# Linear attention and MLP in one kernel: 64-token chunks from the fourth pair on, and a new order of loads, transposes and stores around it

## The chip, the cores and the metric

The kernel runs on one core of a Trainium2 chip. The metric is the device time of one execution in microseconds (us). PE is TensorE, DVE is VectorE, ACT is ScalarE, POOL is GpSimd; SP is the engine whose queue issues most of the transfers.

## The reference, cut to what matters

```python
# q, k, v: (4 batches, 8 heads, 768 tokens, 64); block = 64
for b in range(nb):
    intra = (q_b @ k_b.T * Dmask) @ v_b          # Dmask[i, j] = lam ** (i - j) for i >= j
    inter = (q_b * lam ** (pos + 1)) @ kv_state
    out_b = intra + inter
    kv_state = lam ** block * kv_state + (k_b * lam ** (block - 1 - pos)).T @ v_b
x = out, heads side by side                      # (4, 768, 512)
xn = (x - mean) / sqrt(var + 1e-6) * g_ln
y = x + relu(xn @ w_ch1) @ w_ch2                 # 512 -> 2048 -> 512
```

The block size is a choice of how to compute: any chunk length gives the same result, with more work inside the chunk and fewer states for a longer one.

## The kernel before, in words

The 3,072 rows are cut into 12 *pairs*, u = 0 to 11. A pair is a window of 256 tokens of one batch, two tiles of 128 rows (the index ab); pairs 0 to 3 are the first windows of the four batches, 4 to 7 the second, 8 to 11 the third. "u=3" is therefore the fourth pair. Each pair goes through attention, a norm and the MLP.

**Attention of a pair.** A load brings k, q and v of the pair, 512 KB each in float32. `in_k`, `in_q` and `in_v` cast them to bfloat16 (kq, vb) and scale q and v by powers of lam. kq is transposed to kqT, by PE for u=0 to 2 (`transpose_pe`) and by the DMA for later pairs (`transpose_dma`). Then come the scores (PE), a mask (DVE, mA), AV into the PSUM tiles po, and `inter`, which adds q times the state. The new states come from pk (k times v on PE, `kv` or `kv64`), which DVE sums with the old state and POOL decays to Sn.

**Two forms.** Pairs u < LB use 128-token chunks. Two neighbouring tokens (j) share a partition, so that one packet of a load is 512 B (line 71), and `scores`, `mask`, `av` and `new_state` do the work. Pairs u >= LB use 64-token chunks: loads of 256 KB in 256 B packets (line 75), `scores64` with half the columns, half as many AV matmuls (`av64`), and `states64`, with a state in mid-pair (Smid, cast to Sm by POOL). LB is 6. `rows_of` gives the matching order of the output rows.

**Norm and MLP.** `norm` copies po to x (ACT), takes mean and variance (DVE) and makes xc; `to_xT` transposes xc, from u=2 on by the DMA. An MLP group is one pair: eight `m1` blocks of eight matmuls (line 484) into a PSUM tile pm1, each followed by a relu on ACT (line 487), and eight `m2` blocks of four matmuls (line 522), and then DVE makes the output tile (`finish`, line 543) and SP stores it. [...]

**What sets the order.** Everything is written out by hand in a list `plan` of m1 and m2 blocks. Items 0 to 21 end the MLP of u=0 and u=1; group u=2 starts at item 22, u=3 at 38, u=4 at 54, and so on every 16. `add(n, steps...)` puts steps after item n, and each engine executes its instructions in that order. So do the DMA queues: an instruction on SP that waits holds all that stands behind it on SP. From u=7 on a fixed pattern repeats: `X(u)` holds AV and inter of u-1 and pk, scores and states of u, all at item 57 + 16 (u - 6).

Steps that the change touches: `fill` and `load_one` (loads), `p0` (casts of a pair), `transpose_dma`, `s1` to `s4` (the 128 form, cut into four places between MLP blocks), `X1` and `X2` (the handover from 128 to 64 at u=6), `wind_up` (AV and inter of a pair on its own, with a separate PSUM tile `rest`, till now only for the last pair), `p4` (the two xT transposes), `finish` (stores).

Of the kernel before, what the change touches and what calls it, by code (L numbers as in the profile page):

```python
# [8 lines left out]
BF16 = mybir.dt.bfloat16  # L9
I32 = mybir.dt.int32  # L10
ALU = mybir.AluOpType
# [5 lines left out]
def kernel(  # L17
# [11 lines left out]
    nc = tc.nc  # L29
    B, H, S, D = q.shape  # L30
    C = 128
    W = 2 * C

    NU = B * S // W
    DM = H * D
    DF = moe_w_ch1.shape[1]
    NP = H // 2
# [11 lines left out]
    wk = ctx.enter_context(tc.tile_pool(name="wk", bufs=2))  # L49
# [3 lines left out]

    half = [slice(0, 64), slice(64, 128)]
    XB = 3
    LB = 6

    def mm_tile(shape, dtype, name):
        return ps.tile(shape, dtype, tag="mm", bufs=4, name=name)
# [2 lines left out]
    qkv_in = {}  # L62

    def source(src, u, hs):
        cc, b = divmod(u, B)
        return src[b, hs, cc * W:(cc + 1) * W, :].rearrange("h (p j) d -> p h (j d)", j=2)

    def fill(got, name, u, hs):
        src = dict(k=k, q=q, v=v)[name]
        if u < LB:  # L70
            nc.sync.dma_start(got[:, hs], source(src, u, hs))  # L71
            return
        cc, b = divmod(u, B)
        for j in range(2):
            nc.sync.dma_start(got[:, hs, j * D:(j + 1) * D],
                              src[b, hs, cc * W + j * C:cc * W + (j + 1) * C, :].rearrange("h p d -> p h d"))

    def load_one(u, name):
        got = inp.tile([128, H, 2 * D], F32, tag=name + "in", name=name + "in")
        fill(got, name, u, slice(0, H))  # L80
        qkv_in.setdefault(u, {})[name] = got.rearrange("p h (j d) -> p h j d", j=2)

    def load_window(u, after_pool=False, parts=1):
        got = {name: inp.tile([128, H, 2 * D], F32, tag=name + "in", name=name + "in") for name in "kqv"}
        if after_pool:

            nc.gpsimd.memset(got["k"][:, 0, 0:1], 0.0)
        n = H // parts
        order = [(name, i) for i in range(parts) for name in "kq"] + [("v", i) for i in range(parts)]
        for name, i in order:  # L90
            hs = slice(i * n, (i + 1) * n)
            fill(got[name], name, u, hs)
        qkv_in[u] = {name: f.rearrange("p h (j d) -> p h j d", j=2) for name, f in got.items()}
# [77 lines left out]
    lam_p = const.tile([128, 2, H], F32)  # L171
# [4 lines left out]
    st = {}  # L176
# [12 lines left out]
    def part(a, dst, hs):  # L189

        return dst[:, a, hs.start // 2:hs.stop // 2].rearrange("p a j e d -> p a e j d")

    ALL = slice(0, H)
# [7 lines left out]
    def in_q(u, eng, hs=ALL):  # L201
# [7 lines left out]
        for j in range(2):  # L209
            eng.tensor_tensor(dst[:, :, :, j], src[:, :, :, j],  # L210
                              lq[:, :, :, j:j + 1].to_broadcast([128, n, 2, D]), op=ALU.mult)

    def in_v(u, eng, hs=ALL):
        n = hs.stop - hs.start
        lv = lam_v[:, hs, :, None] if u < LB else lam_p[:, 1, hs, None, None]
        eng.tensor_tensor(st[u]["vb"][:, hs], qkv_in[u]["v"][:, hs], lv.to_broadcast([128, n, 2, D]), op=ALU.mult)  # L216
# [7 lines left out]
                nc.tensor.transpose(tp[:, i, j, :], s["kq"][:, a, p, j], ident)  # L224
        (eng.tensor_copy if eng else nc.scalar.copy)(s["kqT"][:, a, pairs[0]:pairs[0] + n], tp)

    def transpose_dma(u):
        s = st[u]
        s["kqT"] = wk.tile([128, 2, NP, 2, 128], BF16, tag="kqT", bufs=3, name="kqT")
        for a in range(2):  # L230
            nc.sync.dma_start_transpose(s["kqT"][:, a].rearrange("p b j t -> p (b j) t"),
                                        s["kq"][:, a].rearrange("p b j e d -> p (b j e d)"))

    def scores(u, hf, early=False):

# [95 lines left out]
    def mask64(u, e):  # L331
        s = st[u]
        nc.vector.tensor_tensor(s["mA"][:, e], s["sc"][e],  # L333
                                keep64[:, None, None, :].to_broadcast([128, NP, 2, D]), op=ALU.mult)
# [132 lines left out]
    o_of = {}  # L467
# [61 lines left out]
    def rows_of(u):  # L529

        cc, b = divmod(u, B)
        order = "(c p j) d -> j p c d" if u < LB else "(j c p) d -> j p c d"
        return out[b, cc * W:(cc + 1) * W, :].rearrange(order, c=2, j=2)

    def finish(t, a):
        u, ab = divmod(t, 2)
        x, rstd = x_keep[u]
        cc, b = divmod(u, B)
        if ab == 0:
            o_of[u] = wk.tile([128, 2, DM], F32, tag="o", bufs=3, name="o")  # L540
        o = o_of[u]
        rows = rows_of(u)
        nc.vector.scalar_tensor_tensor(o[:, ab], in0=a, scalar=rstd[:, ab:ab + 1], in1=x[:, ab],  # L543
                                       op0=ALU.mult, op1=ALU.add)
        if u == NU - 1:
            for j in range(2):
                nc.sync.dma_start(rows[j][:, ab], o[half[j], ab])
        elif ab == 1:
            for j in range(2):
                nc.sync.dma_start(rows[j], o[half[j]])  # L550

    def finish_half(t, a, z, w):
        u, ab = divmod(t, 2)
# [138 lines left out]
    load_w2(3)  # L692
    in_v(2, nc.gpsimd)
    load_window(3, after_pool=True)
    load_window(4)

    def p0(u, k_eng=None):
        open_window(u)
        in_k(u, k_eng or nc.gpsimd)
        in_q(u, nc.gpsimd)  # L700
        in_v(u, nc.gpsimd)

    def s0(u):
        kv(u, "po")
# [15 lines left out]
    def wind_up(u):  # L720


        s = st[u]
        if u < LB:
            av(u, range(NP))
        else:
            av64(u)
        inter(u, 0, fence=False)
        qT = s["kqT"][:, 1]
        has = [s["S"][ab][1] is not None for ab in range(2)]  # L730
        rest = [ps.tile([128, H, D], F32, tag="sc", bufs=2, name=f"rest{ab}") if has[ab] else None for ab in range(2)]
        for p in range(NP):
            for jq in range(2):
                for e in range(2):
                    ab = 1 - e
                    if s["S"][ab][jq] is not None:
                        nc.tensor.matmul(rest[ab][half[jq], 2 * p + e, :], lhsT=qT[half[e], p, jq, half[ab]],
                                         rhs=s["S"][ab][jq][half[e], p, :],
                                         start=(p == 0), stop=(p == NP - 1), skip_group_check=True)
        s["x"] = xp.tile([128, 2, DM], F32, tag="x", name="x")  # L740
        s["mv"] = xp.tile([128, 2, 2], F32, tag="mv", name="mv")
        s["xc"] = wk.tile([128, 2, DM], BF16, tag="xc", name="xc")
        for ab in range(2):
            x, xh = s["x"][:, ab], s["x"][:, ab].rearrange("p (a e d) -> p a e d", e=2, d=D)
            nc.scalar.copy(x, s["po"][ab].rearrange("p h d -> p (h d)"))
            if has[ab]:

                odd = xh[:, :, 1 - ab]
                nc.vector.tensor_tensor(odd, odd, rest[ab].rearrange("p (a e) d -> p a e d", e=2)[:, :, 1 - ab], op=ALU.add)
            stats = wk.tile([128, 6], F32, tag="stats", name="stats")  # L750
            nc.vector.bn_stats(stats, x)
            nc.vector.bn_aggr(s["mv"][:, ab], stats)
            nc.vector.scalar_tensor_tensor(s["xc"][:, ab], in0=x, scalar=s["mv"][:, ab, 0:1], in1=g_row,
                                           op0=ALU.subtract, op1=ALU.mult)
# [59 lines left out]
    def X(u):  # L814

        if u - 1 < LB:
            av(u - 1, range(NP))
# [25 lines left out]
    def add(at, *steps):  # L843
        after.setdefault(at, []).extend(steps)
# [5 lines left out]
    add(6, (s2, 2))  # L850
    add(8, (s0, 2))
    add(10, (s3, 2))
    add(12, (s4, 2), (p4, 2), (p0, 3, nc.vector), (transpose_dma, 3))
    for n, name in zip((14, 15, 16), "kqv"):
        add(n, (load_one, 5, name))
    add(15, (rstd_of, 2))
    add(17, (p0, 4))
    add(25, (s1, 3))
    add(25, (transpose_dma, 4))
    add(27, (s2, 3))  # L860
    add(28, (p0, 5))
    add(29, (s3, 3))
    add(30, (s4, 3), (p4, 3))
    for n, name in zip((30, 31, 32), "kqv"):
        add(n, (load_one, 6, name))
    add(34, (rstd_of, 3), (make_keep64,))
    add(37, (transpose_dma, 5))
    add(38, (s1, 4))
    add(39, (p0, 6))
    add(40, (s2, 4))  # L870
    add(42, (s3, 4))
    add(44, (s4, 4), (p4, 4))
    add(46, (transpose_dma, 6))
    add(50, (s1, 5), (rstd_of, 4))
    add(53, (s2, 5))
    for j in range(6, NU):
        at = 55 + 16 * (j - 6)
        if j > 6:
            for n, name in zip((23, 21, 19), "kqv"):
                add(at - n, (load_one, j, name))  # L880
            add(at - 13, (p0, j))
            add(at - 8, (transpose_dma, j))
        if j < LB:
            add(at, (s1_s3, j))
            add(at + 4, (s2_s4, j), (p4, j - 1))
        else:
            if j == 6:
                add(at + 1, (X1, j))
                add(at + 5, (X2, j), (p4, j - 1))
            else:  # L890
                add(at + 2, (X, j), (p4, j - 1))
        add(at + 9, (rstd_of, j - 1))
    add(151, (wind_up, NU - 1), (p4, NU - 1))
    add(159, (rstd_of, NU - 1))
# [32 lines left out]
```

## Time and profile before

| | |
|---|---|
| time before, median of 3 | 215.92 us (214.59 to 216.27) |
| span of the profiled execution | 214.9 us |
| PE busy | 201.9 us, 94% |
| DMA, mean | 173 GB/s, 37.13 MB |
| loads of 512 KB, issue to landing | k 6.5, q 8.7, v 7.7 us (5 each) |
| loads of 256 KB, issue to landing | k 3.9, q 5.2, v 5.6 us (14 each) |
| transposes, issue to landing | xT 3.5 us (20), kqT 3.3 us (18) |

The granted PE clock is 0.996 over the span. On the page, a group of instructions has a line number, an engine, an operation, "out<-in" by the program's names and a count, then busy time and mean duration, then the idle time ahead of it and what ended it. A stretch view gives the busy time of each engine between two times. Matmuls are pipelined, so PE's busy time counts a matmul from issue to its modelled end, and neighbouring ones overlap.

### The profile page before, as it was taken

Reading aid. Unit: us, or ns where it says so; the run is one execution under the profiler, and the core shown is the slowest. Engines: PE = TensorE matmul, PEld = TensorE weight load, DVE = VectorE, ACT = ScalarE, POOL = GpSimd, SP = SyncE. Lnnn points to the kernel's source line nnn. Section 1 sums busy time; section 2 is a strip of 40 time slices with the busy share of each in tenths; the row PEclk is TensorE's granted clock in tenths of the full one; section 3 lists DMA queues with packets and bytes.
Section 4 is the critical chain, followed back from the end, with each engine's and each line's share of the span. In section 5 each row is a group of like instructions: output and inputs, shape, how many; then the busy total and the mean of one; then the engine's idle time right before and its main releaser. Section 6 shows DMA issues by size and latency. Waiting matters only on the chain.

```text
span 214.9 us, 6642 instructions
## 1 busy us (share of the span) xinstructions
PE 201.9 (94%) x2884; PEld 138.2 (64%) x2899; DVE 102.9 (48%) x225; ACT 87.1 (41%) x165; POOL 79.4 (37%) x111
## 2 busy tenths in 40 slices
PE   2989999999799999999999999999999999999992
PEld 0568788454674675585585685784784874866861
DVE  3678461565168436747347256174183292522011
ACT  4765679120442244055063162261370460731600
POOL 4747139039464173229019138056065020000000
PEclk9999999999999999999999999999999999999998
DMA  4999999999999898799799999998998511320303
GB/s 130 289 272 207 219 263 160 236 284 234 215 303 208 169 229 153 110 215 209 126 220 199 137 230 200 177 203 198 206 246 131 128 27 27 99 52 0 98 3 95
DMA packets 94142, 37.13 MB, mean 173 GB/s; under 512 B 68385, under 2 KB 91169, under 8 KB 94114
## 3 DMA queue, kind: packets, MB, share of 16 engines
q1 hardware_dynamic: 89584, 32.38, 71.4%
q0 software_dynamic: 4224, 4.19, 12.4%
q8 instruction: 22, 0.36, 0.7%
q10 hardware_dynamic: 306, 0.14, 0.3%
q14 instruction: 6, 0.05, 0.1%
HBM read 27.27 MB, written 6.29 MB: 156 GB/s over the span
## 4 chain that ended last, share of the span: by engine, by line
PE 75%; DMA 13%; POOL 4%; SPq 3%; DVE 2%; issue 1%; POOLq 0%
PE pm L484 35%; PE pm L522 30%; DMA vin<-in_v_dram 6%; DMA qin<-in_q_dram 4%; SPq L71 3%; DMA kqT<-kq 2%; POOL kq L210 2%; POOL vb L216 2%; PE pm2h L513 2%; PE po L406 1%; PE po L393 1%; PE sc L247 1%; PE po L380 1%; PE sc L327 1%; PE pm1t L496 1%
## 5 line engine op out<-in xcount | busy, mean ns | idle before, releaser
L487 ACT ACTIVATE hT<-pm 128x512 bf16<-128x512 f32 x92 | 54.9, 601 | 91.2 <-PE pm L484 91.0
L484 PE MATMUL pm<-xT,w 128*128 128x256 bf16 x736 | 86.3, 273 | 1.9 <-DMA xT<-xc 1.2
L522 PE MATMUL pm<-w,hT 128*128 128x512 bf16 x353 | 81.1, 379 | 1.0 <-issue 0.3
L484 PEld LDWEIGHTS <-w 128*128 128x128 bf16 x736 | 69.8, 98 | 13.8 <-DMA xT<-xc 1.7
L522 PEld LDWEIGHTS <-hT 128*128 128x128 bf16 x368 | 35.5, 98 | 40.0
L543 DVE SCALAR_TENSOR_TENSOR o<-pm,rstd,x 128x512 f32<-128x512 f32 x23 | 17.1, 748 | 43.5 <-PE pm L522 43.4
L287 POOL TENSOR_TENSOR Sn<-Stmp,lam_s 128x256 bf16<-128x256 f32 x16 | 9.7, 611 | 69.7 <-DVE Stmp L365 49.0
L435 DVE SCALAR_TENSOR_TENSOR xc<-po,mv,g_row 128x512 bf16<-128x512 f32 (+1 forms) x24 | 16.8, 706 | 1.8
L257 DVE TENSOR_TENSOR mA<-sc,keep 128x512 bf16<-128x512 f32 x20 | 13.1, 685 | 6.8 <-PE sc L247 6.7
L428 ACT COPY x<-po 128x512 f32<-128x512 f32 x18 | 9.9, 588 | 11.3 <-PE po L393 5.3
L430 DVE BATCH_NORM_STATS2 stats<-x 128x6 f32<-128x512 f32 x18 | 12.4, 688 | 3.9 <-ACT x L428 3.9
L417 DVE COPY seen<-po 128x8 f32<-128x8 f32 x18 | 2.3, 162 | 23.2 <-PE po L406 23.2
L216 POOL TENSOR_TENSOR vb<-vin,lam_v 128x1024 bf16<-128x1024 f32 (+1 forms) x7 | 11.8, 1696 | 3.7 <-DMA vin<-in_v_dram 3.7
L210 POOL TENSOR_TENSOR kq<-qin,lam_q 128x512 bf16<-128x512 f32 x10 | 10.3, 1045 | 7.0 <-DMA qin<-in_q_dram 7.0
L210 POOL TENSOR_TENSOR kq<-qin,lam_p 128x512 bf16<-128x512 f32 x12 | 12.3, 1042 | 0.9 <-DMA qin<-in_q_dram 0.7
L216 POOL TENSOR_TENSOR vb<-vin,lam_p 128x1024 bf16<-128x1024 f32 x6 | 11.4, 1896 | 1.7 <-DMA vin<-in_v_dram 1.7
L199 POOL CAST kq<-kin 128x512 bf16<-128x512 f32 (+1 forms) x18 | 10.3, 599 | 0.6 <-DMA kin<-in_k_dram 0.6
L333 DVE TENSOR_TENSOR mA<-sc,keep 128x512 bf16<-128x512 f32 x12 | 8.2, 681 | 1.4 <-PE sc L327 1.4
L406 PE MATMUL po<-Sn,kqT 64*64 64x64 bf16 x216 | 7.4, 199 | 0.0
L224 PE MATMUL tp<-ident,kq 128*128 128x128 bf16 x48 | 6.2, 277 | 0.3 <-ACT kq L199 0.2
L406 PEld LDWEIGHTS <-kqT 64*64 64x64 bf16 x304 | 5.3, 108 | 1.5 <-issue 1.5
L224 PEld LDWEIGHTS <-kq 128*128 128x128 bf16 x48 | 4.1, 120 | 3.2 <-DVE kq L199 1.5
(98 smaller groups left out, 146.0 us busy)
## 6 DMA issues: line engine op xcount, KB each, us to landing
out_dram<-o SPq DMA_DIRECT2D x22, 256.0 KB, 4.5
w<-in_moe_w_ch_dram POOLq DMA_DIRECT2D x8, 512.0 KB, 9.6
kin<-in_k_dram SPq DMA_DIRECT2D x14, 256.0 KB, 3.9
qin<-in_q_dram SPq DMA_DIRECT2D x14, 256.0 KB, 5.2
vin<-in_v_dram SPq DMA_DIRECT2D x14, 256.0 KB, 5.6
kin<-in_k_dram SPq DMA_DIRECT2D x5, 512.0 KB, 6.5
qin<-in_q_dram SPq DMA_DIRECT2D x5, 512.0 KB, 8.7
vin<-in_v_dram SPq DMA_DIRECT2D x5, 512.0 KB, 7.7
```

What stands on the lines that cost most here:

```text
L199: (eng.copy if eng is nc.scalar else eng.tensor_copy)(dst[:, :, :, j], src[:, :, :, j])
L210: eng.tensor_tensor(dst[:, :, :, j], src[:, :, :, j], lq[:, :, :, j:j + 1].to_broadcast([128, n, 2, D]), op=ALU.mult)
L216: eng.tensor_tensor(st[u]["vb"][:, hs], qkv_in[u]["v"][:, hs], lv.to_broadcast([128, n, 2, D]), op=ALU.mult)
L224: nc.tensor.transpose(tp[:, i, j, :], s["kq"][:, a, p, j], ident)
L257: nc.vector.tensor_tensor(s[f"mA{hf}"][:, e], s[f"sc{hf}"][e], kp[:, None, :, :].to_broadcast([128, 2, 2, 128]), op=ALU.mult)
L406: nc.tensor.matmul(s["po"][ab][half[jq], 2 * p + e, :], lhsT=qT[half[e], p, jq, half[ab]], rhs=s["S"][ab][jq][half[e], p, :], start=False, ...
L430: nc.vector.bn_stats(stats, po if early else x)
L435: nc.vector.scalar_tensor_tensor(xc[:, sl], in0=po[:, sl], scalar=mv[:, 0:1], in1=g_row[:, sl], op0=ALU.subtract, op1=ALU.mult)
L484: nc.tensor.matmul(pm[:, b, :], lhsT=w1[n // W2K][:, kk, (n % W2K) * 128:(n % W2K + 1) * 128], rhs=xT_of[g][:, kk, 0:N], start=(b == 0 and ...
L487: nc.scalar.activation(hT[:, u * NB:(u + 1) * NB, 0:N], pm, ACT.Relu)
L522: nc.tensor.matmul(acc[i], lhsT=hT[:, kk, i * 128:(i + 1) * 128], rhs=w2[kk // W2K][:, kk % W2K, :], start=(kk == 0), stop=(kk == KB - 1))
L543: nc.vector.scalar_tensor_tensor(o[:, ab], in0=a, scalar=rstd[:, ab:ab + 1], in1=x[:, ab], op0=ALU.mult, op1=ALU.add)
```

## The change

LB goes from 6 to 3, so u=3, 4 and 5 take the 64 form, with its loads. The schedule from item 11 to item 57 is rewritten for it. The loads of u=4 are no longer issued together with those of u=3; its k is issued from ACT's queue, its q and v from SP's behind the transposes of u=3's kq and of u=2's xc. u=3's k is cast by ACT. Its AV and inter are done by `wind_up`, u=3's and u=4's pk, scores and states by a new `first64`, which has u=4's q cast in two halves between them, one on POOL and one on DVE. The stores of u=0 to 2 are taken out of `finish` and issued at items 34 and 40. The aim is less attention work on PE in the stages of the MLP that carry u=3 to u=5, with the transposes that PE waits for ahead of loads that are needed later.

```diff
-    LB = 6
+    LB = 3
...
-    def load_one(u, name):
+    def load_one(u, name, eng=None):
...
+    def in_q_one(u, eng, j):
+        src = qkv_in[u]["q"].rearrange("p (a e) j d -> p a e j d", e=2)
+        lq = lam_p[:, 0, :].rearrange("p (a e) -> p a e", e=2)
+        eng.tensor_tensor(part(1, st[u]["kq"], ALL)[:, :, :, j], src[:, :, :, j],
+                          lq[:, :, :, None].to_broadcast([128, NP, 2, D]), op=ALU.mult)
...
-    def transpose_dma(u):
...
-        for a in range(2):
-            nc.sync.dma_start_transpose(s["kqT"][:, a].rearrange("p b j t -> p (b j) t"),
-                                        s["kq"][:, a].rearrange("p b j e d -> p (b j e d)"))
+    def transpose_dma(u, a):
...
+        nc.sync.dma_start_transpose(s["kqT"][:, a].rearrange("p b j t -> p (b j) t"),
+                                    s["kq"][:, a].rearrange("p b j e d -> p (b j e d)"))
...
-        elif ab == 1:
-            for j in range(2):
-                nc.sync.dma_start(rows[j], o[half[j]])
+        elif ab == 1 and u > 2:
+            store(u)
...
-    load_window(4)
...
+    def first64(u, ahead=None):
+        kv64(u)
+        scores64(u)
+        if ahead is not None:
+            in_q_one(ahead, nc.gpsimd, 0)
+        mask64(u, 0)
+        states64(u, 0)
+        if ahead is not None:
+            in_q_one(ahead, nc.vector, 1)
+        mask64(u, 1)
+        states64(u, 1)
...
-                nc.vector.tensor_tensor(odd, odd, rest[ab].rearrange("p (a e) d -> p a e d", e=2)[:, :, 1 - ab], op=ALU.add)
+                rows = slice(0, 128) if s["S"][ab][0] is not None else half[1]
+                nc.vector.tensor_tensor(odd[rows], odd[rows], rest[ab].rearrange("p (a e) d -> p a e d", e=2)[rows, :, 1 - ab], op=ALU.add)
...
-    add(12, (s4, 2), (p4, 2), (p0, 3, nc.vector), (transpose_dma, 3))
-    for n, name in zip((14, 15, 16), "kqv"):
-        add(n, (load_one, 5, name))
+    add(11, (open_window, 3), (in_k, 3, nc.scalar), (in_q, 3, nc.gpsimd))
+    add(12, (s4, 2), (make_keep64,), (in_v, 3, nc.gpsimd), (load_one, 4, "k", nc.scalar))
+    add(12, (transpose_dma, 3, 0), (to_xT, 2, 0), (transpose_dma, 3, 1), (to_xT, 2, 1))
+    add(12, (load_one, 4, "q"), (load_one, 4, "v"))
     add(15, (rstd_of, 2))
-    add(17, (p0, 4))
-    add(25, (s1, 3))
-    add(25, (transpose_dma, 4))
-    add(27, (s2, 3))
-    add(28, (p0, 5))
-    add(29, (s3, 3))
-    add(30, (s4, 3), (p4, 3))
-    for n, name in zip((30, 31, 32), "kqv"):
-        add(n, (load_one, 6, name))
-    add(34, (rstd_of, 3), (make_keep64,))
-    add(37, (transpose_dma, 5))
-    add(38, (s1, 4))
-    add(39, (p0, 6))
-    add(40, (s2, 4))
-    add(42, (s3, 4))
-    add(44, (s4, 4), (p4, 4))
-    add(46, (transpose_dma, 6))
-    add(50, (s1, 5), (rstd_of, 4))
-    add(53, (s2, 5))
-    for j in range(6, NU):
+    add(20, (open_window, 4), (in_k, 4, nc.vector))
+    add(21, (first64, 3, 4))
+    add(22, (transpose_dma, 4, 0), (transpose_dma, 4, 1), (load_one, 5, "k"), (load_one, 5, "q"))
+    add(23, (in_v, 4, nc.gpsimd))
+    add(28, (wind_up, 3), (p4, 3), (load_one, 5, "v"))
+    add(28, (open_window, 5), (in_k, 5, nc.gpsimd), (transpose_dma, 5, 0))
+    add(30, (first64, 4))
+    add(32, (in_q, 5, nc.gpsimd), (in_v, 5, nc.gpsimd))
+    add(34, (rstd_of, 3), (transpose_dma, 5, 1), (store, 0), (store, 1))
+    add(40, (store, 2))
+    for j in range(5, NU):
...
-        if j > 6:
-            for n, name in zip((23, 21, 19), "kqv"):
+        if j > 5:
+            for n, name in zip((17, 16, 15) if j == 6 else (23, 21, 19), "kqv"):
...
-            else:
-                add(at + 2, (X, j), (p4, j - 1))
+        add(at + (4 if j == 5 else 2), (X, j), (p4, j - 1))
```

More of the change, by code (lines that the diff above doesn't have):

```diff
@@ L66, in source, with fill @@
         return src[b, hs, cc * W:(cc + 1) * W, :].rearrange("h (p j) d -> p h (j d)", j=2)
-    def fill(got, name, u, hs):
+    def fill(got, name, u, hs, eng=None):
+        eng = eng or nc.sync
         src = dict(k=k, q=q, v=v)[name]
         if u < LB:
-            nc.sync.dma_start(got[:, hs], source(src, u, hs))
+            eng.dma_start(got[:, hs], source(src, u, hs))
             return
@@ L74, in fill @@
         for j in range(2):
-            nc.sync.dma_start(got[:, hs, j * D:(j + 1) * D],
-                              src[b, hs, cc * W + j * C:cc * W + (j + 1) * C, :].rearrange("h p d -> p h d"))
-    def load_one(u, name):
+            eng.dma_start(got[:, hs, j * D:(j + 1) * D],
+                          src[b, hs, cc * W + j * C:cc * W + (j + 1) * C, :].rearrange("h p d -> p h d"))
+    def load_one(u, name, eng=None):
         got = inp.tile([128, H, 2 * D], F32, tag=name + "in", name=name + "in")
-        fill(got, name, u, slice(0, H))
+        fill(got, name, u, slice(0, H), eng)
         qkv_in.setdefault(u, {})[name] = got.rearrange("p h (j d) -> p h j d", j=2)
@@ L225, in transpose_pe @@
         (eng.tensor_copy if eng else nc.scalar.copy)(s["kqT"][:, a, pairs[0]:pairs[0] + n], tp)
-    def transpose_dma(u):
+    def transpose_dma(u, a):
         s = st[u]
-        s["kqT"] = wk.tile([128, 2, NP, 2, 128], BF16, tag="kqT", bufs=3, name="kqT")
-        for a in range(2):
-            nc.sync.dma_start_transpose(s["kqT"][:, a].rearrange("p b j t -> p (b j) t"),
-                                        s["kq"][:, a].rearrange("p b j e d -> p (b j e d)"))
+        if "kqT" not in s:
+            s["kqT"] = wk.tile([128, 2, NP, 2, 128], BF16, tag="kqT", bufs=3, name="kqT")
+        nc.sync.dma_start_transpose(s["kqT"][:, a].rearrange("p b j t -> p (b j) t"),
+                                    s["kq"][:, a].rearrange("p b j e d -> p (b j e d)"))
     def scores(u, hf, early=False):
@@ L547, in finish, with store @@
                 nc.sync.dma_start(rows[j][:, ab], o[half[j], ab])
-        elif ab == 1:
-            for j in range(2):
-                nc.sync.dma_start(rows[j], o[half[j]])
+        elif ab == 1 and u > 2:
+            store(u)
+    def store(u):
+        for j in range(2):
+            nc.sync.dma_start(rows_of(u)[j], o_of[u][half[j]])
     def finish_half(t, a, z, w):
@@ L877 @@
+    add(40, (store, 2))
+    for j in range(5, NU):
         at = 55 + 16 * (j - 6)
-        if j > 6:
-            for n, name in zip((23, 21, 19), "kqv"):
+        if j > 5:
+            for n, name in zip((17, 16, 15) if j == 6 else (23, 21, 19), "kqv"):
                 add(at - n, (load_one, j, name))
             add(at - 13, (p0, j))
[L882 to L885, printed above, removed]
-        else:
[L887 to L890, printed above, removed]
-                add(at + 2, (X, j), (p4, j - 1))
+            add(at - 8, (transpose_dma, j, 0), (transpose_dma, j, 1))
+        add(at + (4 if j == 5 else 2), (X, j), (p4, j - 1))
```

## The prediction

> **What bounds the kernel now.** I read the page's busy shares and slices first, then the span cut into stages, then the timeline of PE, then that of SP's queue.
>
> ```profile
> PE 201.9 (94%) x2884; PEld 138.2 (64%) x2899; DVE 102.9 (48%) x225; ACT 87.1 (41%) x165; POOL 79.4 (37%) x111
> DMA  4999999999999898799799999998998511320303
> ```
>
> Two resources are near full: PE over the whole span, and the DMA engines up to about 160 us. Every other engine is under half. The stages begin where the first matmuls of a pair's MLP begin (columns: stretch, length, then PE, PEld, DVE, ACT, POOL busy, clock, DMA share, GB/s):
>
> ```profile
> 55.02:72.02 17.00, 16.57 (x239) 10.79 (x241) 7.78 (x17) 6.24 (x11) 7.56 (x11) 1.00 0.98 222
> 72.02:89.93 17.91, 17.66 (x319) 11.63 (x322) 10.55 (x22) 5.94 (x11) 7.54 (x9) 1.00 0.97 178
> 89.93:106.11 16.18, 15.91 (x258) 10.75 (x259) 8.85 (x19) 6.10 (x11) 6.92 (x9) 1.00 0.89 178
> 106.11:121.47 15.36, 15.31 (x225) 10.47 (x225) 7.77 (x17) 6.05 (x11) 6.88 (x9) 1.00 1.09 188
> 121.47:136.69 15.22, 15.17 (x217) 10.50 (x217) 7.35 (x16) 6.05 (x11) 6.37 (x8) 1.00 1.03 197
> ```
>
> The MLP of one pair is the same work in each. Stages with attention in 128-token chunks take 16.2 to 17.9 us, those in 64-token chunks 15.2 to 15.4. PE is filled in all of them, so the difference is PE work and PE's breaks. The one long PE wait after the head is just ahead of this table:
>
> ```profile
> 55.02 3.65 PE L484 MATMUL pm<-xT,w 128*128 128x256 bf16 x32 [1.20 <-DMA xT<-xc]
> ```
>
> It waits for u=2's xT, and SP's queue says why: the loads of u=4 stand ahead of those transposes (start, length, line[...]).
>
> ```profile
> 47.05 1.93 SPq L71 DMA_DIRECT2D vin<-in_v_dram  x1
> 49.08 3.64 SPq L451 DMA_TRANSPOSE xT<-xc  x2
> 52.82 2.62 SPq L231 DMA_TRANSPOSE kqT<-kq  x2
> ```
>
> **What the Trainium skill says.** "DMA: Bandwidth & Descriptors", Specifications, puts the smallest transfer for full rate at 512 B. The trace agrees: with 512 B packets the queue moved 310 GB/s (43 to 45.5 us), with 256 B packets 228 GB/s (95 to 97.5). The same page, Anatomy of one DMA, gives about 2 us fixed, mostly the write receipt, for transfers from GpSimd's queue. On SP's queue a 256 KB k load onto a quiet queue landed 3.4 to 3.7 us after issue; 1.15 us is data at 228 GB/s and 0.6 us issue, so about 2 us remain here too. Its section "Issuing engines are not separate DMA queues" says that loads from ACT's queue run on the same 16 engines; the trace of before has no large load there, so I give u=4's k no bandwidth of its own.
>
> **The change, part by part.**
>
> *PE.* u=3, 4 and 5 go from stages of 17.00, 17.91 and 16.18 us to about 15.25: 1.75 + 2.66 + 0.93 = 5.3 us less. Cross-check in the chain of waits: per pair the 128 form has scores 2 x 0.35, AV 0.64, pk 0.38; the 64 form scores 0.29, AV 0.38, pk 0.32, and the inter matmuls stay 32. That is 0.7 us a pair, 2.2 in three. The rest is fewer places where attention cuts the MLP's stream (16 L484 matmuls between two cuts take 1.85 us, in an unbroken run of 32 they take 1.75) and small waits (0.2 to 0.3 us each at pk, scores and relu). I take 5.3, with 2.2 as the low end.
>
> *DVE and POOL.* The 128 form asks of DVE two Stmp sums (0.42) and four masks (0.68), 3.6 us; the 64 form two Smid, two Stmp (0.42 each) and two masks, 3.1. POOL gains two Sm casts (0.40). Neither is near full, so nothing. u=4's second q half moves to DVE. No row shows it; L210 on DVE at half the size took 0.42, so 0.7 us, at most POOL's 1.04. u=3's k casts go to ACT: 2 x 0.66 beside PE's m2 run, where ACT is idle. make_keep64 and the half-height add are hidden likewise.
>
> *Loads.* Three sets of 1.57 MB change from 512 B to 256 B packets: 5.1 us to 6.9, so 1.8 each and 5.4 us more queue work before about 75 us. Stores of 2 KB rows are unchanged in size.
>
> *Order of SP's queue.* u=4's loads no longer stand ahead of xT(2); u=4's q and v now stand behind. Hand reckoning: at 42.3 the weights end and 679 packets of u=3 have moved; the other 5,465 of the new 6,144 need 6.1 us, to 48.4; q lands about 48.2 against 46.7 now. POOL's q casts end near 49.3, kqT(3)'s second transpose is issued then, xT(2)'s second at 50.7 (each issue 1.2 to 1.3 us). Behind 48.4 the engines still have u=4's k (2.3 us), two kqT (2.6, their issue time) and two xT of half the size (1.3): to 54.6, landing 55 to 56. Now: 55.02. So the **1.20 us wait stays, roughly**: I take 55.3.
>
> *New wait.* In first64(3), DVE's q half for u=4 stands ahead of mask64(3, 1) and states64(3, 1). That q is issued behind xT(2), data to 56.9, landing 58.9. Until then DVE holds; behind it are the mask and sums, 2.2 us with the q half itself, to 61.1, and POOL's decay and cast to 62.1. wind_up(3) comes seven m1 blocks after 55.3, at 61.4, and wants the last state 0.4 us later: a wait of **0.3 us**. If instead the two PSUM tiles pk are wanted by the third m1 (57.1) before DVE has read them (60.7), PE waits **3.6 us**. In the present sixth-to-seventh handover the fourth m1 after pk is the first whose wait is on DVE's reads (it ran unhindered), so I take the small value.
>
> *Later.* kqT(4) goes out at 59.7 to 61, u=5's k and q data run to 65.8, xT(3) about 66 to 69, v to 72, kqT(5) is issued by 73.9 and lands 75.9; X(5) starts at 55.3 + 15.4 + 5.2 = 75.9, so no wait. But then stores 0 and 1 (3.4 us), u=6's k and q (4.6), store 2 (1.7) and v (2.3) put the data of xT(4) at 86.2, landing about 88.5, and PE wants it at 55.3 + 30.7 = 86.0: 2.5 us. kqT(6) and v of u=6 stand behind the same queue: about 1 more. From u=7 on the queue has slack (1.6 us of 115 to 130 us are idle slices), so the queue recovers.
>
> *Sum.* Saved 5.3. Given back between 0 (every transfer in time) and 0.3 + 0.3 + 2.5 + 1.0 = 4.1. The reckoning charges every transfer one after the other and no overlap of transposes with loads, so I take the middle, about 2.2: 215.9 - 5.3 + 2.2 = **212.8 us**.
>
> **The rivals.**
>
> 1. *All transfers are in time*, and the 1.20 us wait goes too, as u=4's loads are gone from ahead of xT(2). For it: the queue has idle slices around 70 to 73 and 83 to 92 us now, about 9 us that could be filled. Against: PE runs 5 us ahead of those slices. 215.9 - 5.3 - 1.2 = 209.4 us.
> 2. *The DMA queue becomes the bound* up to u=6, as in the full reckoning: 215.9 - 5.3 + 4.1 = 214.7 us, hardly a change. For it: the DMA row is at 9 nearly everywhere; 5.4 us of work are added and 5.3 us of time removed. Against: 1.6 us of each later stage are idle.
> 3. *Slower*: DVE held by u=4's q also holds the pk tiles (3.6 us), SP sits at kqT(4) behind it and everything after is late by as much again. 215.9 - 5.3 + 3.6 + 4.1 = 218.3 us. For it: one late q stalls DVE, POOL's second half and SP together. Against: the handover above reuses pk late, and the PE and queue delays overlap in part.
>
> **How the numbers follow.** My forecast 0.40, rival 1 0.22, rival 2 0.23, rival 3 0.15. The 1% bounds are 213.8 and 218.1. Faster: 0.36 of the forecast, rival 1's 0.22, 0.03 of rival 2: 0.61. Same: 0.04, 0.18 of rival 2 and 0.02 of rival 3: 0.24. Slower: 0.02 and 0.13: 0.15. The range runs from rival 1, 209.2, to 217.4, which leaves out rival 3's slower half and little else.
>
> **What would show it.** Right: the stages of u=2, 3 and 4's MLP near 15.3 us each, L247 and L393 at half their counts, 256 KB loads at 20 issues each for k, q and v (14 now, two more a pair). For the forecast against rival 1: PE still waits about a microsecond for xT or kqT near 55 us, and 1 to 3 us for xT(4) or kqT(6) near 86 to 89. Rival 3 shows as PE idle near 57 us, released by DVE (Smid) with DVE itself released by the qin load. The prediction is wrong if the three stages stay above 16 us with PE full, or if the queue of u=6 lands before PE asks.

## The result, and the profile after

The changed kernel takes 230.11 us (median; 228.61 to 231.08) against 215.54 us: the ratio is 1.066, 95% interval 1.061 to 1.072. It is slower by 14.6 us. The forecast was 212.8 us, and even its slower rival stopped at 218.3. Some executions fall into a slower state of the chip: the ratios here compare fast executions alone, the medians take in all of them.

From the page of the kernel after, the busy shares and three of the rows (tenths of 40 slices; PEclk is the granted clock):

```profile
PE 203.4 (89%) x2811; PEld 139.4 (61%) x2811; DVE 104.4 (46%) x227; ACT 87.9 (38%) x167; POOL 79.9 (35%) x115
PE   2969999999779996029999999999999999999993
PEclk9999999999999999656999999999999999999999
DMA  5999999999997799059989889899797532330303
```

One hole in PE, near 90 us, with a slow clock after it. PE is idle from 89.5 to 101.2 us, and in the slice from 91.4 to 97.1 us the DMA row is 0: for half of the wait no transfer is running that PE could be waiting for. The stages, cut as before at the first m1 matmul of each pair's MLP (same columns):

```profile
55.25:73.92 18.67, 15.77 (x225) 10.50 (x217) 12.14 (x24) 6.05 (x11) 9.06 (x13) 1.00 0.88 175
73.92:101.25 27.33, 15.61 (x225) 10.57 (x224) 8.32 (x18) 6.05 (x11) 10.18 (x12) 0.85 0.62 145
101.25:119.33 18.08, 18.08 (x224) 11.88 (x225) 7.02 (x16) 6.05 (x11) 6.88 (x9) 0.85 1.09 185
119.33:134.60 15.27, 15.24 (x225) 10.35 (x224) 7.78 (x17) 6.05 (x11) 6.88 (x9) 1.00 0.98 190
```

Before, these three stages took 17.00, 17.91 and 16.18 us; now 18.67, 27.33 and 18.08. PE is busy only 15.6 of the 27.3 us of the second stage: the time is a wait. In the third it is busy throughout and still takes 2.8 us more than in the next: that is the clock, 0.50 over the first 3.3 us:

```profile
101.20:104.50 3.30, 3.25 (x16) 2.36 (x17) 0.00 (x0) 0.60 (x1) 0.00 (x0) 0.50 1.36 124
```

The busy times of a stage before and after are not the same work: the pk and scores of u=3, for one, lay in the first stage before and now stand ahead of it.

The chain of waits that ended last, in order of time (start, length, what), read from the loads of u=6 to PE:

```profile
87.40 4.45 DMA vin<-in_v_dram
...
91.98 1.90 POOL vb L223
93.88 0.58 POOL Sn L294
...
94.48 0.43 DVE Smid L369
...
97.94 0.38 DVE xc L442
...
98.72 2.40 DMA xT<-xc
...
101.25 6.37 PE pm L491 x32
```

And the timeline of POOL and of DVE over the same time, with the idle time ahead of each instruction and what ended it:

```profile
85.34 0.61 POOL L200 CAST kq<-kin 128x512 bf16<-128x512 f32 x1 [8.27 <-DMA kin<-in_k_dram]
...
91.98 1.90 POOL L223 TENSOR_TENSOR vb<-vin,lam_p 128x1024 bf16<-128x1024 f32 x1 [2.79 <-DMA vin<-in_v_dram]
93.83 0.61 POOL L294 TENSOR_TENSOR Sn<-Stmp,lam_s 128x256 bf16<-128x256 f32 x1
```

```profile
81.20 0.68 DVE L340 TENSOR_TENSOR mA<-sc,keep 128x512 bf16<-128x512 f32 x1
94.48 0.42 DVE L369 TENSOR_TENSOR Smid<-pk,Sn 128x256 f32<-128x256 f32 x1 [12.60 <-POOL Sn L294]
```

The decay of u=5's state (Sn, POOL) needs a sum that DVE had ready at 81.3 us. It ran at 93.83, as the casts of u=6 stand ahead of it on POOL, and their last load landed at 91.9. DVE, in its own order, has the norm of u=4 behind that state; so xc, xT and PE's next stage wait too. In the schedule this is one line: p0 of u=6 is at item 42 and X(5) at item 43. From u=7 on X(u) is at 57 + 16 (u - 6) and the casts of the pair after it one item later; the change put X(5) two items later than this pattern and left the casts of u=6 where the pattern has them.

### The profile page after: what moved, and what is told of

Its sections match the earlier page's. It is cut to its first block, busy times and chain, and to the rows that moved or that the text cites. A ratio compares the mean times of both kernels' runs of the same rounds, so it can differ in the third digit from the quotient of the medians.

```text
span 228.4 us, 6502 instructions
## 1 busy us (share of the span) xinstructions
PE 203.4 (89%) x2811; PEld 139.4 (61%) x2811; DVE 104.4 (46%) x227; ACT 87.9 (38%) x167; POOL 79.9 (35%) x115
## 4 chain that ended last, share of the span: by engine, by line
PE 67%; DVE 9%; DMA 9%; SPq 7%; POOL 3%; ACT 2%; issue 1%; DVEq 0%; POOLq 0%
PE pm L491 31%; PE pm L529 25%; DMA kin<-in_k_dram 4%; SPq L76 3%; PE pm1t L503 2%; DMA qin<-in_q_dram 2%; DMA vin<-in_v_dram 2%; SPq L560 2%; SPq L72 2%; PE pm2h L520 2%; DVE xc L442 1%; DVE stats L437 1%; PE tp L231 1%; PE po L387 1%; DMA xT<-xc 1%
## 5 line engine op out<-in xcount | busy, mean ns | idle before, releaser
L491 PE MATMUL pm<-xT,w 128*128 128x256 bf16 x736 | 88.2, 278 | 13.3 <-DMA xT<-xc 11.7
L491 PEld LDWEIGHTS <-w 128*128 128x128 bf16 x736 | 71.8, 100 | 26.0 <-issue 13.9
L223 POOL TENSOR_TENSOR vb<-vin,lam_p 128x1024 bf16<-128x1024 f32 x9 | 17.1, 1897 | 3.0 <-DMA vin<-in_v_dram 3.0
L211 POOL TENSOR_TENSOR kq<-qin,lam_p 128x512 bf16<-128x512 f32 x16 | 16.4, 1042 | 2.0 <-DMA qin<-in_q_dram 2.0
L442 DVE SCALAR_TENSOR_TENSOR xc<-po,mv,g_row 128x512 bf16<-128x512 f32 (+1 forms) x22 | 15.3, 702 | 1.7
L369 DVE TENSOR_TENSOR Smid<-pk,Sn 128x256 f32<-128x256 f32 x17 | 7.2, 423 | 14.2 <-POOL Sn L294 12.6
L340 DVE TENSOR_TENSOR mA<-sc,keep 128x512 bf16<-128x512 f32 x18 | 12.3, 681 | 0.0
L437 DVE BATCH_NORM_STATS2 stats<-x 128x6 f32<-128x512 f32 x16 | 11.0, 685 | 0.8 <-ACT x L435 0.8
L468 ACT ACTIVATE std<-mv,eps_t 128x2 f32<-128x2 f32 x12 | 3.6, 299 | 19.5 <-DVE mv L438 16.5
L264 DVE TENSOR_TENSOR mA<-sc,keep 128x512 bf16<-128x512 f32 x8 | 5.2, 686 | 6.3 <-PE sc L254 6.3
L377 POOL CAST Sm<-Smid 128x256 bf16<-128x256 f32 x18 | 7.6, 423 | 1.0 <-DVE Smid L369 1.0
```

The costliest lines, as they stand in the source:

```text
L211: eng.tensor_tensor(dst[:, :, :, j], src[:, :, :, j], lq[:, :, :, j:j + 1].to_broadcast([128, n, 2, D]), op=ALU.mult)
L340: nc.vector.tensor_tensor(s["mA"][:, e], s["sc"][e], keep64[:, None, None, :].to_broadcast([128, NP, 2, D]), op=ALU.mult)
L437: nc.vector.bn_stats(stats, po if early else x)
L442: nc.vector.scalar_tensor_tensor(xc[:, sl], in0=po[:, sl], scalar=mv[:, 0:1], in1=g_row[:, sl], op0=ALU.subtract, op1=ALU.mult)
L491: nc.tensor.matmul(pm[:, b, :], lhsT=w1[n // W2K][:, kk, (n % W2K) * 128:(n % W2K + 1) * 128], rhs=xT_of[g][:, kk, 0:N], start=(b == 0 and ...
```

## The experiments

All ratios are against the kernel before, run on the same chip. Profiles of kernels with the same instructions up to item 11 reach the end of item 21 anywhere from 53.5 to 57 us, so I compare stages and waits, and medians of the timed runs, not single spans.

**e1: the casts of u=6 behind X(5).**

```diff
-            add(at - 13, (p0, j))
+            add(at - (11 if j == 6 else 13), (p0, j))
```

> One line moves: the casts of u=6 (p0) go from item 42, ahead of X(5), to item 44, behind it. Theory A (POOL's order: u=5's decay stands behind casts of u=6 whose loads land up to 92 us, DVE waits for the decay and xc of u=4 behind it): the 11.7 us wait of PE for xT shrinks to 3 us or less, what is left being xT behind the loads of u=6 on SP; the slow m1 stretch after it (6.4 us for 32 matmuls in place of 3.7) goes as well; 215 to 218 us, against 230. Theory B (SP's queue is too late by itself, the order on POOL is not what counts): xT still lands past 98 us, 224 us or more.

222.13 us, ratio 1.023 (1.015 to 1.032). Over the kernel before, 14.6 us have become 6.3 by the medians (215.79 on this chip) and 5.0 by the ratio: 8 to 9.5 us are gone by moving one step two items. The time is above theory A's numbers and below B's. PE's wait fell to 3.6 us, a little more than A's 3, and the clock still fell after it (0.52 from 94.0 to 97.4 us); timeline of PE, from the first m1 of u=2 and from that of u=4:

```profile
58.01 6.51 PE L491 MATMUL pm<-xT,w 128*128 128x256 bf16 x56 [1.68 <-DMA xT<-xc]
...
94.04 5.21 PE L491 MATMUL pm<-xT,w 128*128 128x256 bf16 x32 [3.64 <-DMA xT<-xc]
```

**e12: the decay on DVE, POOL's order as in the change.** This takes the link away from the other side: every transfer and cast stays in its place.

```diff
-            decay(nc.gpsimd, Sn, tmp)
+            decay(nc.vector if u == 5 else nc.gpsimd, Sn, tmp)
```

> The changed kernel, casts of u=6 left ahead of X(5) on POOL, but u=5's two decays on DVE in place of POOL: the same transfers in the same order, without DVE's wait for POOL. Theory A (DVE held by POOL held by the loads): as e1, PE's wait for xT of u=4 falls from 11.7 to 3 to 4 us, 221 to 224 us. If the loads or SP's order hold xT by themselves: 228 us or more.

223.58 us, ratio 1.035 (1.029 to 1.041); the same two places:

```profile
58.31 6.42 PE L491 MATMUL pm<-xT,w 128*128 128x256 bf16 x56 [0.65 <-DMA xT<-xc]
...
94.66 5.32 PE L491 MATMUL pm<-xT,w 128*128 128x256 bf16 x32 [3.78 <-DMA xT<-xc]
```

Two edits that share nothing but the removed wait of DVE for POOL bring PE's wait to the same 3.6 to 3.8 us, and the intervals of their ratios overlap. Theory A is shown for this part of the loss, 8 to 9.5 us of 14.6.

**e2: the stores early again, POOL's order as in the change.**

```diff
-        elif ab == 1 and u > 2:
+        elif ab == 1:
             store(u)
...
-    add(34, (rstd_of, 3), (transpose_dma, 5, 1), (store, 0), (store, 1))
-    add(40, (store, 2))
+    add(34, (rstd_of, 3), (transpose_dma, 5, 1))
```

> Undoes the late stores alone: stores of u=0 to 2 go out in finish again, the casts of u=6 stay ahead of X(5). Theory A: the loads of u=6 are issued 3 to 5 us earlier, as SP has no stores ahead of them, POOL's casts and so the decay come earlier by as much, and PE's wait falls from 11.7 to 7 to 9 us: 224 to 227 us. Theory C (late stores are needed to get the early transposes through): kqT of u=4 and xT of u=3 come late behind stores, PE waits near 66 to 74 us, no gain or a loss: 230 to 233 us.

228.22 us, ratio 1.059 (1.051 to 1.067), between the two forecasts; the interval overlaps that of the change itself (1.061 to 1.072), so the gain in time is not clear of noise. In the trace both things happened:

```profile
67.68 0.44 PE L334 MATMUL sc<-kqT 64*64 64x64 bf16 x32 [2.32 <-DMA kqT<-kq]
...
99.19 6.35 PE L491 MATMUL pm<-xT,w 128*128 128x256 bf16 x32 [9.30 <-DMA xT<-xc]
```

The wait for xT of u=4 fell from 11.7 to 9.3 us: the loads of u=6 have the store of one pair ahead of them in place of those of two or three, and are issued 0.8 to 1.7 us earlier. And kqT of u=4, now behind the stores of u=0 and 1, made PE wait 2.3 us for the scores near 65 us. Late stores did what they were meant to do, and their price came later.

**e4: e1 and e2 together.**

> e1 and e2 together: casts of u=6 behind X(5), stores of u=0 to 2 in finish. Theory A: with both gone from ahead of xT(4), PE's wait for it is under 1 us, and what is left are the waits of 1.5 us (pk) and 1.4 us (scores of u=4): 212 to 215 us. If the queue is the bound whatever the order: no better than e1.

218.48 us, ratio 1.012 (1.008 to 1.015), between the two forecasts, the lowest of the full kernels with the new form, and still slower than before. The wait near 90 us is down to 0.4 us. The long waits that are left are early; PE's timeline:

```profile
58.22 0.45 PE L334 MATMUL sc<-kqT 64*64 64x64 bf16 x32 [2.66 <-DMA kqT<-kq]
...
63.35 2.78 PE L491 MATMUL pm<-xT,w 128*128 128x256 bf16 x24 [0.81 <-DVE Smid L369]
...
69.96 0.44 PE L334 MATMUL sc<-kqT 64*64 64x64 bf16 x32 [0.98 <-DVE x L771]
```

**e3: the 256 B packets alone, on the kernel before.**

```diff
         if u < LB:
-            nc.sync.dma_start(got[:, hs], source(src, u, hs))
+            if u < 3:
+                nc.sync.dma_start(got[:, hs], source(src, u, hs))
+                return
+            cc, b = divmod(u, B)
+            for j in range(2):
+                nc.sync.dma_start(got[:, hs, j * D:(j + 1) * D],
+                                  src[b, hs, cc * W:(cc + 1) * W, :].rearrange("h (p j) d -> j p h d", j=2)[j])
```

> The kernel before with the loads of u=3 to 5 cut in two halves of 256 B packets, all else kept: the disputed cost of the packets by itself. Hand reckoning (5.4 us more queue work, the queue near full to 70 us): the 1.20 us wait for xT at 55 us grows to 3 to 5 us and part of it stays to the end: 217 to 221 us. If the packets are hidden: within 1 us of 215.5.

222.51 us, ratio 1.030 (1.024 to 1.035), above both forecasts: the smaller packets of three pairs, and the two load instructions in place of one that come with them, cost 6.7 us when the schedule stays as it was. 4.9 us of this appear as two waits of PE for xT, that of u=2 (1.20 us before) and that of u=3 (none before); the rest is not placed:

```profile
58.79 3.65 PE L490 MATMUL pm<-xT,w 128*128 128x256 bf16 x32 [3.07 <-DMA xT<-xc]
...
78.82 1.03 PE L490 MATMUL pm<-xT,w 128*128 128x256 bf16 x8 [3.07 <-DMA xT<-xc]
```

**e7 and e9: the new form without its packets.** e7 is e4 with 512 B packets for u=3 to 5; those pairs' tokens are then taken in another order than the reference's. e9 also puts both q halves of u=4 behind the states of u=3, and first64(4) at item 31.

```diff
-        if u < LB:
+        if u < 6:
             eng.dma_start(got[:, hs], source(src, u, hs))
```

> e4 with u=3 to 5 loaded in the 512 B packets of the 128-token layout; the 64-token form then works on tokens in another order, so the time is that of the change without its packets. If the packets are what eats the gain (e3: 6.7 us on the kernel before): 210 to 213 us, with stages of 15.3 us and no long wait of PE. If the 64-token form or the new order costs by itself: 216 us or more.

> e7 (512 B packets for u=3 to 5) with both q halves of u=4 behind the masks and sums of u=3, and first64(4) at item 31: no transfer and no cast stands ahead of the states of u=3. If the waits of DVE and POOL for q were what kept e7 from the gain: the stage of u=2's MLP falls from 18.2 to 16.5 us or less and the time to 212 to 215 us. If those waits move on to xT of u=3 (kqT of u=4 comes later): the stage stays near 18 and the time near e7's 217.

e7: 217.4 us, ratio 1.003 (1.000 to 1.006), in the range of the second theory: without the small packets there is still no gain. Against e4 the packets are worth 0.9% in this schedule, about 1.9 us, and not 6.7 (e10 below against e9: 1.9%, about 4.2 us). PE waits 1.5 us for Smid behind u=4's q, 0.8 us for the scores of u=4 and 1.25 us for xT of u=4. e9: 215.6 us, ratio 0.999 (0.996 to 1.002), between the forecasts. Its stages, from the starts of m1 in its timeline, are 17.66, 15.36 and 15.60 us, against 17.00, 17.84 and 16.08 before, read from starts as well. The first holds a new wait, for xT of u=3, whose transposes now stand behind kqT of u=4:

```profile
56.40 0.45 PE L353 MATMUL pk<-vb,kq 64*64 64x64 bf16 x32
56.68 0.44 PE L334 MATMUL sc<-kqT 64*64 64x64 bf16 x32
57.05 6.32 PE L491 MATMUL pm<-xT,w 128*128 128x256 bf16 x56
...
74.71 5.40 PE L491 MATMUL pm<-xT,w 128*128 128x256 bf16 x48 [1.79 <-DMA xT<-xc]
```

Less that wait the three stages sum to 46.8 us in place of 50.9. But the pk and scores of u=3, which lie in the first stage before, stand ahead of it here, from 56.40 to 57.05 us. With these 0.65 us counted, the saving on PE is 3.4 us, half of it taken back by the wait in the first stage. What is left of it is not seen in the whole time: PE comes to these steps at 56.4 us in this profile and at 53.8 in that of before. As such starts differ by 3.5 us between profiles with the same early instructions, it is open whether the change has a part in that.

**e5, e6, e10: other orders of the early part, on e4.** e5 puts DVE's q half last and first64(4) at item 32; e6 loads u=4's k from SP's queue; e10 makes e9's two moves.

```diff
         mask64(u, 0)
         states64(u, 0)
-        if ahead is not None:
-            in_q_one(ahead, nc.vector, 1)
         mask64(u, 1)
         states64(u, 1)
+        if ahead is not None:
+            in_q_one(ahead, nc.vector, 1)
...
-    add(30, (first64, 4))
+    add(32, (first64, 4))
```

> e4 and two moves: DVE's q half of u=4 behind the masks and sums of u=3, and first64(4) from item 30 to 32, behind the read of the PSUM tile rest. If the two waits of PE in e4 (0.8 us for Smid, 1.0 us for the read of rest) count: 216.5 to 217.5 us against e4's 218.5. If they are absorbed by a later wait for transfers: 218 to 219 us.

> e4 (256 B packets) with the same two moves. With the queue as the bound the removed waits come back at xT or kqT: 217.5 to 220 us. If the order on DVE and POOL is the bound: 215 to 217 us.

> e4 with the k of u=4 on SP's queue, behind the transposes. If the k on ACT's queue takes DMA time from the transposes ahead of PE's first wait: kqT of u=3 lands 1 to 2.5 us sooner and PE's wait of 2.7 us for it shrinks; DVE's k casts come later, so part is lost again: 216.5 to 219 us. If the k is better early (as the change supposes): PE waits for DVE (k casts ahead of the masks of u=3) and 220 us or more.

e5: 219.98 us (ratio 1.012 to 1.027), above both forecasts. e10: 219.69 (1.013 to 1.024), as its first forecast says. The waits for Smid and for the read of rest are gone from both, and came back as waits for transfers; in e10 kqT of u=4 is issued after the later q cast:

```profile
67.79 0.45 PE L334 MATMUL sc<-kqT 64*64 64x64 bf16 x32 [2.54 <-DMA kqT<-kq]
68.17 7.04 PE L529 MATMUL pm<-w,hT 128*128 128x512 bf16 x24
```

e6: 222.42 us (1.024 to 1.037). PE no longer waits for kqT of u=3, as the first forecast said, but 1.4 us for xT of u=2, and then 2.6 us for DVE, which holds for the k casts. The time is the second forecast's: the k on ACT's queue is worth its place.

**e8 and e11: parts of the change on the kernel before.** e8 issues the loads of u=4 behind xT of u=2 and kqT of u=3. e11 gives one pair, u=5, the 64-token form.

```diff
-    load_window(4)
...
     add(12, (s4, 2), (p4, 2), (p0, 3, nc.vector), (transpose_dma, 3))
+    for name in "kqv":
+        add(12, (load_one, 4, name))
...
-    add(17, (p0, 4))
     add(25, (s1, 3))
-    add(25, (transpose_dma, 4))
+    add(26, (p0, 4))
+    add(26, (transpose_dma, 4))
```

> The kernel before with one idea of the change: the loads of u=4 are issued behind xT of u=2 and kqT of u=3, and its casts on POOL follow at item 26. If PE's 1.20 us wait for xT is owed to those loads: it goes, 214 to 215 us. If the later casts and kqT of u=4 cost as much again: 215.5 to 218 us.

```diff
-    LB = 6
+    LB = 5
...
-    add(30, (s4, 3), (p4, 3))
+    add(30, (s4, 3), (p4, 3), (transpose_dma, 5))
...
-    add(37, (transpose_dma, 5))
     add(38, (s1, 4))
-    add(39, (p0, 6))
     add(40, (s2, 4))
-    add(42, (s3, 4))
-    add(44, (s4, 4), (p4, 4))
-    add(46, (transpose_dma, 6))
-    add(50, (s1, 5), (rstd_of, 4))
-    add(53, (s2, 5))
+    add(43, (X, 5), (p4, 4))
+    add(44, (p0, 6))
+    add(47, (transpose_dma, 6))
+    add(48, (rstd_of, 4))
...
```

> The kernel before with one pair more in the 64-token form (u=5 alone, LB = 5), X(5) at item 43, kqT of u=5 ahead of the loads of u=6, and the casts of u=6 behind X(5) on POOL. Only one set of loads has 256 B packets, in a stretch where the queue has idle slices now. If the gain of the form is real and only the early packets and the order on POOL ate it: 213.5 to 215 us, the stage of u=4's MLP near 15.3 us in place of 16.1. If the form gains nothing in place: 216 us or more.

e8: 221.33 us (1.019 to 1.029), above both forecasts: the wait of 1.20 us went, and xT of u=3 came 3.9 us late behind the displaced loads. e11: 221.04 us (1.019 to 1.029), a miss. Its stage of u=4's MLP is 15.36 us as forecast, but PE waits 1.7 us for xT of u=3 ahead of that pair's stage, and the stage takes 19.6 us, with a gap in the middle of an m1 block for which the trace names no releaser:

```profile
81.94 1.27 PE L484 MATMUL pm<-xT,w 128*128 128x256 bf16 x10
85.64 0.83 PE L484 MATMUL pm<-xT,w 128*128 128x256 bf16 x6 [2.43 <-issue]
```

No version beat the kernel before.

## Why the prediction was wrong

**The step that failed** is the one that said "X(5) starts at 55.3 + 15.4 + 5.2 = 75.9, so no wait", and the wait of "2.5 us" for xT of u=4 after it. I followed X(5) through SP's queue and never through POOL's. The matmuls of X(5) did start without a wait, at 79.3 us; its decay stood behind casts of u=6. That term was 2.5 us and measured 11.7. e1 and e12 show the cause. The part on DVE and POOL has the same fault: it sets both at nothing because "Neither is near full". POOL was busy 35% of the span and still held the decay for 12.5 us (81.3 to 93.8), by the order of its instructions.

**A term that was missing** is the clock. In the stage after the wait 32 m1 matmuls took 6.37 us in place of 3.7, so the wait cost 2.7 us more. The Trainium skill, "TensorE: Matmul & The Clock Gate", Part 1, says that the clock falls to half after an idle window of about 3.4 us and comes back after one of sustained work. For the waits for xT the runs agree. After 3.07 us (e3) the 32 matmuls took 3.65; after 3.64 (e1) 5.21; after 3.78 (e12) 5.32; after 9.30 (e2) 6.35; after 11.73 6.37. But e10 differs: there the clock fell after a wait of 2.54 us. The 24 m2 matmuls after it took 7.04 us (5.35 in e9), with a clock of 0.51 in their middle:

```profile
70.00:72.00 2.00, 2.00 (x6) 0.66 (x5) 0.49 (x2) 0.00 (x0) 1.83 (x4) 0.51 1.24 224
```

In e6 it fell too, after waits of 1.44 and 2.57 us with one m1 block between them (0.55 from 61.5 to 64.8 us). So the length of one wait does not decide it; what else does is open here.

Point by point, the rest:

- PE's saving, 5.3 us: mis-sized. By the stages alone it is 4.1 us in e9, as they take 15.9 (less the wait), 15.4 and 15.6 us and not 15.25 each; with u=3's pk and scores, which only moved ahead of them, it is 3.4. The low end, 2.2, was too low.
- The wait for xT of u=2 "stays, roughly", m1 at 55.3 us: it began at 55.25, which is luck. In this profile there is no wait: xT was there when PE came. In e1 and e12, which have the same instructions on every queue up to item 42, m1 waited 1.68 and 0.65 us for xT and began at 58.0 and 58.3.
- DVE held by u=4's q: the mechanism was right. The q half began at 58.35 us (58.9 forecast for the landing) and took 1.14 us (0.7 forecast). PE waited 1.53 us for Smid, between the two ends given (0.3 and 3.6), at the fifth m1 and not the third. In e1 and e12, where PE came later, this wait does not show.
- Not seen: 1.36 us at the scores of u=4. They take the same PSUM tiles as the `rest` of `wind_up`, which DVE reads in the norm of u=3. In the kernel before `wind_up` ran once, at the end, with nothing behind it.
- Queue work of 256 B packets, 5.4 us: e3 measured 6.7 us of time (222.51 less 215.79) in the old schedule; in the new ones it was 1.9 and 4.2 (e4 against e7, e10 against e9). That the queue is near its bound (rival 2) fits e5, where removed waits return as waits for transposes. In e10 the transposes also stand behind a later cast, so the queue's share is not separated there.
- Rival 3 had the right side, and the wrong place for it: not near 57 us, but at 82 to 94, by the same pattern of an engine held by a load ahead of a short step.

The account of 14.6 us: 8 to 9.5 go with POOL's order (e1) and about 3 more with the stores once POOL's order is right (e4: 3.6 by the medians, 2.5 by the ratios, whose intervals just touch; PE's wait for xT falls from 3.64 to 0.40 us). The remaining 2.5 to 2.7 are placed in part: in e4's profile the stretch from PE's first step after item 21 to the first m1 of u=5 is 1.1 us longer than before, its waits less the saving on PE, and the rest lies outside it. That the two shares belong to these steps holds in this order of removal; taken first, the stores were worth 1.9 by the medians (e2), which is not clear of noise.

The same stretch of the changed kernel closes the sum. It is 12.6 us longer than before, 64.7 against 52.1 us: 11.7 for xT of u=4, 2.7 of slow clock, 1.5 and 1.4 for the two early waits, less the 1.2 of the wait that went, make 16.1; so PE's work is 3.5 us less, in agreement with e9.

**Open:** the gap without a releaser in e11 (83.2 to 85.6 us); smaller ones (0.2 us before, 1.0 in e7) stand at similar places. The trace has a lead. Among its DMA queues is one of kind "instruction", with transfers of 16 KB, and one of these starts at 82.9 us. In each of the eleven profiles with such a gap in an m1 block, one starts 2.4 to 3.4 us ahead of the gap's end. That fits PE waiting for its next instructions while loads fill the DMA engines, but no run tested it.

## What to carry to other kernels

Where a schedule is written by hand, check each moved step against every in-order queue that it enters, not only the one that the change is about: ask what stands ahead of it there, and what that waits for. A cast that waits for a load must not stand ahead of a short step on a chain that another engine needs next. And a smaller amount of work on the bound engine pays only if its inputs can come as early: here the form gained about 3.5 us on PE and needed smaller packets, which cost 6.7 us in the old schedule and 1.9 to 4.2 in the new ones.

## What the runs showed of the hardware

A wait of PE for data can cost more than its length. After waits of 3.64 us (e1) and 2.54 us (e10) the matmuls that followed took 1.6 and 1.7 us longer, with the clock near half; after one of 3.07 us (e3) nothing was lost. The same three pairs' bytes in 256 B in place of 512 B packets, with twice as many load instructions, cost 6.7 us of a time of 216, although no more bytes moved.
